# Two-stage token mix on one core: another entry into the first round, paced adds of x, DRAM adds moved, casts shared

## The chip, the cores and the metric

The kernel runs on one core of a Trainium2 chip. The metric is device time in microseconds. A core has a matrix engine (TensorE, called PE in the profile, with its weight loads as PEld), a vector engine (VectorE, DVE), an activation engine (ScalarE, ACT), GpSimd (POOL) and a queue engine (SyncE, SP). Each runs its own instructions in order; they meet only in semaphores. Transfers are issued by SP, ACT and POOL.

## The reference

The input x has shape (8, 4224, 192): batch, sequence, channels. First comes a causal convolution over 7 positions with softmax weights per head. Its result, called x again, goes through a mix of channels, a mix of tokens and another mix of channels:

```python
theta = x @ w_theta
zr, zi = x * cos(theta), x * sin(theta)
y = einsum('ts,bsd->btd', w_tok_r, zr) + einsum('ts,bsd->btd', w_tok_i, zi)
u = x + y
out = u + maximum(u @ w_ch, 0)
```

The token mix is by far the largest part: two matrices of 4224 x 4224, each applied to 1536 columns (batch times channel).

## The kernel before, in words

**Tiles.** The source tokens are cut into NK = 33 chunks of 128, the target tokens into NT = 33 blocks of 128. Two blocks make a unit, so there are NU = 17 units, the last with one block. In a pair, a scheme with seven products in place of eight is used: the weights of a pair of blocks give the tiles "11", "12", "21", "22" (turned by DVE, line 329) and the sums S1 to S4 (DVE, line 341); the chunk's z gives matching tiles Z11, T1, T2 and so on (products at line 248, sums at line 254).

**Steps.** The kernel is a sequence of NSTEP = 58 steps. A step works on one unit and on all chunks that are active in it. Chunk k is active for 17 steps from `start[k]`, so it meets every unit once. At most NW = 11 chunks are active at a time: the 33 chunks pass in three rounds of 11. `base` says in which step of its round each chunk enters, and `self.n` is the number of active chunks of a step:

```python
base = [0, 0, 1, 1, 2, 3, 3, 4, 4, 5, 5]
start = [base[k % NW] + (NU + 1) * (k // NW) for k in range(NK)]
```

In the first steps n is therefore 2, 4, 5, 7, 9, 11. A step has seven runs, one for each product tile; a run is n pairs of matmuls (line 429). After a run, `give` adds the PSUM result into the block's partial sum pv, on DVE (line 394), or copies it there on ACT (line 392) where it is a first visit. There are two PSUM tiles for the runs, so a later run waits until an earlier one has been given. Partial sums go to DRAM (`part`, two arrays used in turn) at the end of a step and come back when their unit is next visited (`load_rows`, line 365).

**A chunk's way in.** `load_chunk` fetches x (POOL queue, line 194, and SP for the overlap with the chunk before, line 185). `conv` is PE with ACT (lines 207, 148), and writes x to the DRAM array `xs`. `transpose` goes over PE; the copy out of PSUM is DVE's for chunks 0 to 2, ACT's for later ones. `theta` is PE (line 138) and two sines on ACT (line 243). Then come `product` and `sums` on DVE.

**The order** is written out by hand. Each engine's instructions are chained in program order. Inside a step, `mix` takes events (time in units of a run, action) and issues them between the pairs. The weights of step t+1 are turned and summed during step t (`w_tasks`: turns at 0.25, 1.2, 2.2, 4.2, sums at 2.05, 3.05, 3.3, 5.1). Their loads from DRAM (`load_w`, POOL, line 316) are issued in step t-1, into two stage buffers `st`, one for each weight matrix, so a load waits until the turns that read the buffer before it are done.

**The head** is the loop over i in the last part of the kernel. It brings in chunks 0 to 10, issues chunk i's convolution and chunk i-1's theta, products and sums, and fills in up to 11 pairs of the mix per iteration (`more`), as far as their chunks are ready; in iterations 1 and 2 it also issues matmuls on zeros (`idle`, line 571). The weights of step 0 are turned in iteration 1, ahead of the first transposed chunk's products:

```python
steps[0].load_rows()
for m in (1, 2):
    steps[0].load_w(m)
load_chunk(2)
for m in (1, 2):
    steps[1].load_w(m)
```

**Adding x.** u = x + y needs x added once to every block. For 24 blocks `add_x` loads x into xr (SP, line 375) and POOL adds it to pv in SBUF (line 376). For 9 blocks that are finished in the last steps (`self.late`) POOL issues accumulating transfers from `xs` into `part` in DRAM (line 381, two halves each), four steps before the block's last visit.

**The end of a block.** In its last visit pv is cast to 16 bits (ACT, line 451), transposed by a crossbar transfer issued by ACT (`cross_u`, line 155), or over PE in the late steps, multiplied by w_ch on PE (line 138), combined on DVE (line 464) and sent out by SP.

Of the kernel before, what the change touches and what calls it, by code (L numbers as in the profile page):

```python
# [9 lines left out]
AT = mybir.ActivationFunctionType  # L10
# [6 lines left out]
def kernel(  # L17
# [43 lines left out]
    NW = 11  # L61
    PC = 512

    base = [0, 0, 1, 1, 2, 3, 3, 4, 4, 5, 5]
    assert len(base) == NW
# [4 lines left out]
    NOSYNC = mybir.DependencyInfo(  # L70
        mybir.DependencyClass.NoSync, mybir.DependencyReason.DATA
    )
    last = {}

# [207 lines left out]
    class Step:  # L282


        def __init__(self, t):
            self.t, self.u, self.ks = t, unit(t), active(t)
            self.n = len(self.ks)
            self.tbs = [tb for tb in (2 * self.u, 2 * self.u + 1) if tb < NT]
            self.pair = len(self.tbs) == 2
            self.first = t < NU  # L290
            self.final = t + NU >= NSTEP
            self.late = self.final and self.n < NW
            self.ahead = self.late or 0 <= t + NU - NSTEP < 2
            visits = [v for v in range(NU, NSTEP) if v % NU == t % NU]
            self.adds = []
# [7 lines left out]
            self.st, self.w, self.ub, self.uT, self.pv = {}, {}, {}, {}, []  # L303

        def known(self, tb):

# [51 lines left out]
        def load_rows(self):  # L358
            for tb in self.tbs:
# [7 lines left out]
                    )  # L367
                self.pv.append(pv)

        def add_x(self, i):  # L370

            rows = slice(self.tbs[i] * P, (self.tbs[i] + 1) * P)
            if not self.ahead:
                xr = wk.tile([P, N], F16, name="xr", tag="xr", bufs=1)
                nc.sync.dma_start(out=xr, in_=xs[rows, :])
                pool(nc.gpsimd.tensor_tensor(  # L376
                    out=self.pv[i], in0=self.pv[i], in1=xr, op=ALU.add
                ))
                return
# [66 lines left out]
        def cast(self, i, g):  # L446
            if g == 0:
                self.ub[i] = wk.tile([P, N], F16, name="ub", tag="ub", bufs=2)
                self.uT[i] = turned()
            cols = slice(g * GC, (g + 1) * GC)  # L450
            act(nc.scalar.activation(  # L451
                out=self.ub[i][:, cols], in_=self.pv[i][:, cols], func=AT.Copy
            ))

        def turn_u(self, i, g):
            transposed(self.uT[i], self.ub[i], [g])
# [268 lines left out]
```

## Time and profile before

| What | Value |
|---|---|
| time, median of 9 runs | 1463.19 us |
| lowest and highest | 1455.8 and 1468.85 us |
| profiled execution, its own time | 1455.8 us |
| its span, first to last instruction | 1454.0 us |
| PE busy | 1418.5 us, 98% of the span |
| DVE busy | 1017.5 us, 70% |
| POOL busy | 435.6 us, 30% |
| ACT busy | 317.4 us, 22% |
| mean granted TensorE clock | 0.997 |
| DMA | 281.98 MB, mean 194 GB/s |

A busy engine is one with an instruction in flight. PE can be busy and still slow, since its matmuls overlap: the mean of one in a row is its latency, and the rate is read from how many there are in a stretch. A row of the page names line, engine, operation, output and inputs, shape and count; after the bar come the busy time, the mean of one in ns, the idle time of the engine just before and what ended it. In a timeline a row is start, length, engine, line, operation, count, and in brackets the idle time before it and its releaser. A window row gives, for each engine, the busy time in that stretch and in parentheses the number of instructions.

### The profile page before, as it was taken

Reading aid. Unit: us, or ns where it says so; the run is one execution under the profiler, and the core shown is the slowest. Engines: PE = TensorE matmul, PEld = TensorE weight load, DVE = VectorE, ACT = ScalarE, POOL = GpSimd, SP = SyncE. Lnnn points to the kernel's source line nnn. Section 1 sums busy time; section 2 is a strip of 40 time slices with the busy share of each in tenths; the row PEclk is TensorE's granted clock in tenths of the full one; section 3 lists DMA queues with packets and bytes.
Section 4 is the critical chain, followed back from the end, with each engine's and each line's share of the span. In section 5 each row is a group of like instructions: output and inputs, shape, how many; then the busy total and the mean of one; then the engine's idle time right before and its main releaser. Section 6 shows DMA issues by size and latency. Waiting matters only on the chain.

```text
span 1454.0 us, 23744 instructions
## 1 busy us (share of the span) xinstructions
PE 1418.5 (98%) x9809; PEld 888.3 (61%) x9809; DVE 1017.5 (70%) x1048; ACT 317.4 (22%) x382; POOL 435.6 (30%) x655
## 2 busy tenths in 40 slices
PE   7899999999999999999999999999999999999997
PEld 4556666666666666666656556666566666666565
DVE  6893554555458687867777757876788688677585
ACT  5861101111134244000000004335200100110134
POOL 8431211111223322532322443233133123234220
PEclk9999999999999999999999999999999999999999
DMA  9986756564699999897878889989889999999984
GB/s 172 233 174 139 145 116 134 98 151 89 153 229 210 223 236 241 207 260 152 242 167 195 225 147 242 227 197 237 211 184 209 214 200 205 235 255 205 252 207 139
DMA packets 272028, 281.98 MB, mean 194 GB/s; under 512 B 106672, under 2 KB 240176, under 8 KB 271920
## 3 DMA queue, kind: packets, MB, share of 16 engines
q0 software_dynamic: 162464, 92.15, 48.2%
q1 hardware_dynamic: 71824, 178.88, 35.2%
q10 hardware_dynamic: 37632, 9.44, 4.5%
q8 instruction: 77, 1.26, 0.3%
q14 instruction: 31, 0.25, 0.1%
HBM read 245.49 MB, written 108.13 MB: 243 GB/s over the span
## 4 chain that ended last, share of the span: by engine, by line
PE 85%; DVE 6%; DMA 3%; ACT 2%; issue 1%; POOL 1%; DVEq 0%; SPq 0%; ACTq 0%; POOLq 0%
PE y L429 78%; PE v L138 5%; DVE wt L341 2%; PE pc L207 1%; DMA uT<-ub 1%; PE tp L162 1%; ACT z L243 1%; DVE pv L394 1%; DVE wt L329 1%; DMA xw<-in_x_dram 1%; DVE z L254 1%; POOL st L316 1%; DVE z L248 1%; ACT uT L148 0%; DMA xs<-z 0%
## 5 line engine op out<-in xcount | busy, mean ns | idle before, releaser
L429 PE MATMUL y<-z,wt 128*128 128x384 f16 x7656 | 1285.0, 326 | 12.9 <-DVE pv L394 9.7
L429 PEld LDWEIGHTS <-wt 128*128 128x128 f16 x7656 | 741.0, 98 | 491.8 <-issue 14.2
L394 DVE TENSOR_TENSOR pv<-y,pv 128x768 f32<-128x768 f32 x324 | 308.5, 953 | 299.2 <-PE y L429 259.7
L329 DVE STREAM_TRANSPOSE wt<-st 128x1408 f16<-128x1408 f16 (+7 forms) x224 | 327.8, 1465 | 45.8 <-PE y L429 39.1
L316 POOL DMA_DIRECT2D st<-in_moe_w_tok_r_dram x232 | 132.8, 579 | 465.4 <-DVE wt L329 449.9
L316 POOL DMA_DIRECT2D st<-in_moe_w_tok_i_dram x232 | 132.7, 579 | 465.2 <-DVE wt L329 448.8
L341 DVE TENSOR_TENSOR wt<-wt 128x1408 f16<-128x1408 f16 (+7 forms) x216 | 218.8, 1013 | 40.7 <-PE y L429 38.2
L148 ACT ACTIVATE z<-pc 128x768 f16<-128x768 f32 x65 | 53.2, 819 | 389.4 <-PE pc L207 389.1
L451 ACT ACTIVATE ub<-pv 128x768 f16<-128x768 f32 x66 | 52.5, 836 | 343.7 <-DVE pv L394 327.5
L392 ACT ACTIVATE pv<-y 128x768 f32<-128x768 f32 x66 | 54.0, 818 | 281.8 <-PE y L429 281.8
L138 PEld LDWEIGHTS <-uT 128*128 128x128 f16 x1056 | 91.5, 98 | 29.5 <-issue 8.0
L194 POOL DMA_DIRECT2D xw<-in_x_dram x132 | 76.3, 584 | 28.1 <-DMA xw<-xw 7.7
L464 DVE SCALAR_TENSOR_TENSOR pv<-v,pv 128x768 f32<-128x768 f32 x66 | 62.8, 953 | 24.3 <-PE v L138 22.8
L376 POOL TENSOR_TENSOR pv<-pv,xr 128x1536 f32<-128x1536 f32 x24 | 74.7, 3111 | 17.1 <-issue 12.1
L254 DVE TENSOR_TENSOR z<-z 128x768 f16<-128x768 f16 x132 | 73.4, 556 | 3.6
L148 ACT ACTIVATE uT<-tp 128x1536 f16<-128x1536 f16 (+1 forms) x48 | 58.2, 1215 | 66.3 <-PE tp L162 66.3
L243 ACT ACTIVATE z<-v,half_pi 128x768 f16<-128x768 f32 x66 | 59.8, 906 | 41.9 <-PE v L138 41.5
L248 DVE TENSOR_TENSOR z<-z 128x1536 f16<-128x1536 f16 x66 | 60.0, 948 | 7.1 <-ACT z L243 7.1
L138 PE MATMUL v<-wch,uT 128*128 128x192 f16 x528 | 54.9, 248 | 4.8 <-DMA uT<-ub 2.9
L138 PE MATMUL v<-wth,uT 128*128 128x192 f16 x528 | 55.0, 248 | 4.5 <-ACT z L243 3.0
L243 ACT ACTIVATE z<-v 128x768 f16<-128x768 f32 x66 | 53.4, 810 | 0.0
L207 PE MATMUL pc<-xw,bands 96*64 96x192 f16 x528 | 35.5, 257 | 2.3 <-ACT bands L614 1.1
(43 smaller groups left out, 140.8 us busy)
## 6 DMA issues: line engine op xcount, KB each, us to landing
part<-pv SPq DMA_DIRECT2D x79, 768.0 KB, 4.2
pv<-part SPq DMA_DIRECT2D x79, 768.0 KB, 6.0
out_dram<-pv SPq DMA_DIRECT2D x66, 384.0 KB, 5.2
st<-in_moe_w_tok_r_dram POOLq DMA_DIRECT2D x136, 176.0 KB, 5.8
st<-in_moe_w_tok_i_dram POOLq DMA_DIRECT2D x136, 176.0 KB, 4.8
xs<-z SPq DMA_DIRECT2D x132, 96.0 KB, 4.4
xw<-in_x_dram POOLq DMA_DIRECT2D x121, 96.0 KB, 6.2
xr<-xs SPq DMA_DIRECT2D x24, 384.0 KB, 4.5
```

The source lines that it names most:

```text
L138: pe(nc.tensor.matmul(v[:, k, b * D : (b + 1) * D], lhsT=tT[:, 3 * k + b + i, :], rhs=w[:, 2 * b + i, :], start=(i == 0), stop=(i == 1),))
L148: act(nc.scalar.activation(out=out, in_=in_, func=AT.Copy))
L194: nc.gpsimd.dma_start(out=self.xw[lo : lo + n, h, :, :], in_=x[:, t0 : t0 + n, :].rearrange("b s d -> s b d"),)
L243: act(nc.scalar.activation(**args))
L248: dve(nc.vector.tensor_tensor(out=o, in0=xv, in1=o, op=ALU.mult))
L254: dve(nc.vector.tensor_tensor(out=z[:, o, :], in0=z[:, a, :], in1=z[:, b, :], op=ALU.subtract))
L316: pool(nc.gpsimd.dma_start(out=st[a * Q : (a + 1) * Q, 0:nb, :, 0:n] .rearrange("i r bt s -> i (r bt) s"), in_=w[self.tbs[0] * P : (self.t ...
L329: dve(nc.vector.transpose(self.w[name][:, 0 : self.n, :, :], self.st[int(name[1])][:, int(name[0]) - 1, :, 0 : self.n * Q] .rearrange("p b ...
L341: dve(nc.vector.tensor_tensor(out=self.w[name][:, 0 : self.n, :, :], in0=self.w[a][:, 0 : self.n, :, :], in1=self.w[b][:, 0 : self.n, :, : ...
L376: pool(nc.gpsimd.tensor_tensor(out=self.pv[i], in0=self.pv[i], in1=xr, op=ALU.add))
L394: dve(nc.vector.tensor_tensor(out=o, in0=yv, in1=o, op=ALU.add))
L429: pe(nc.tensor.matmul(y[cn][:, q, 0:BH], lhsT=self.w[wn][:, c, :, :].rearrange("p bt i -> p (bt i)"), rhs=chunks[k].z[:, zn, q * BH : (q + ...
```

## The change

There are five edits.

1. `base` has a list for each round. The first round enters over five steps, three chunks at once in the first (n is 3, 5, 7, 9, 11); the second has another order of its six steps. NSTEP stays 58.
2. Ahead of the head's loop, x of chunk 2 is fetched before step 0's weights, and x of chunk 3 before step 1's. Step 0's weights are turned at the end of iteration 1, after the sums of chunk 0.
3. POOL's add of x in SBUF is split from the load of xr, and given a semaphore wait on the DVE instruction that precedes it in program order; both are issued at other points of the step.
4. The accumulating transfers into DRAM are issued elsewhere: for blocks whose x is complete by step 23, in steps 27 to 35 and into the array that is read one visit earlier; for the others in step 41.
5. In the last two steps the cast of the first half of pv goes to DVE.

```diff
-    base = [0, 0, 1, 1, 2, 3, 3, 4, 4, 5, 5]
-    start = [base[k % NW] + (NU + 1) * (k // NW) for k in range(NK)]
+    base = [[0, 0, 0, 1, 1, 2, 2, 3, 3, 4, 4],
+            [0, 0, 1, 1, 2, 2, 3, 3, 4, 4, 5],
+            [0, 0, 1, 1, 2, 3, 3, 4, 4, 5, 5]]
+    start = [base[k // NW][k % NW] + (NU + 1) * (k // NW) for k in range(NK)]
...
-            self.ahead = self.late or 0 <= t + NU - NSTEP < 2
+            quiet = [v for v in visits if start[2 * NW - 1] < v <= 2 * NU]
+            self.adds, self.ahead = [], []
             for i, tb in enumerate(self.tbs):
-                at = [v for v in visits if self.known(tb) < v - 1 and v + NU < NSTEP
-                      and NU + 1 + base[-1] < v <= 2 * NU]
-                at = at[0] if at else visits[-1]
-                if t == at:
-                    self.adds.append(i)
+                known = self.known(tb)
+                if t not in ([v for v in quiet if known < v - 1] or visits[-1:])[:1]:
+                    continue
+                if not self.late:
+                    self.adds.append(i)
+                else:
+                    far = known <= start[2 * NW - 1]
+                    self.ahead.append((i, 2 * NU - NW + 2 * (t % NU) if far else start[-1],
+                                       (t // NU - 1 - far) % 2))
...
+        def load_x(self, i):
+            self.xr[i] = wk.tile([P, N], F16, name="xr", tag="xr", bufs=1)
+            nc.sync.dma_start(
+                out=self.xr[i], in_=xs[self.tbs[i] * P : (self.tbs[i] + 1) * P, :]
+            )
         def add_x(self, i):
+            ins = pool(nc.gpsimd.tensor_tensor(
+                out=self.pv[i], in0=self.pv[i], in1=self.xr[i], op=ALU.add
+            ))
+            tc.add_manual_dep(ins.ins, last["dve"].ins.name, SYNC, reason="pace")
+        def add_ahead(self, i, which):
+            tb = self.tbs[i]
             for cols in (slice(0, HN), slice(HN, N)):
                 pool(nc.gpsimd.dma_start(
-                    out=part[(self.t // NU - 1) % 2][self.tbs[i], :, cols],
-                    in_=xs[rows, cols], accum_op=ALU.add,
+                    out=part[which][tb, :, cols], in_=xs[tb * P : (tb + 1) * P, cols],
+                    accum_op=ALU.add,
                 ))
...
-            act(nc.scalar.activation(
-                out=self.ub[i][:, cols], in_=self.pv[i][:, cols], func=AT.Copy
-            ))
+            evacuate(self.ub[i][:, cols], self.pv[i][:, cols], self.t >= NSTEP - 2 and g == 0)
...
-            if not steps[t + 1].ahead:
-                for i in steps[t + 1].adds:
-                    found.append((3.3 + 1.7 * i, lambda i=i: steps[t + 1].add_x(i)))
-        for s in steps[t:]:
-            if s.ahead and t == s.t - (4 if s.late else 10):
-                for i in s.adds:
-                    found.append((3.3 + 1.7 * i, lambda s=s, i=i: s.add_x(i)))
+            for i in steps[t + 1].adds:
+                found.append((2 + 2 * i, lambda i=i: steps[t + 1].load_x(i)))
+                found.append((3.6 + 2 * i, lambda i=i: steps[t + 1].add_x(i)))
+        here = [(r, i, which) for r in steps for i, when, which in r.ahead if when == t]
+        for j, (r, i, which) in enumerate(here):
+            found.append((1.5 + 1.8 * j, lambda r=r, i=i, which=which: r.add_ahead(i, which)))
...
     steps[0].load_rows()
+    load_chunk(2)
     for m in (1, 2):
         steps[0].load_w(m)
-    load_chunk(2)
+    load_chunk(3)
     for m in (1, 2):
         steps[1].load_w(m)
...
-        if i == 1:
-            for _, f in steps[0].w_tasks():
-                f()
         if i + 3 < NW:
             load_chunk(i + 3)
...
             old.sums(1)
+        if i == 1:
+            for _, f in steps[0].w_tasks():
+                f()
         between(1)
```

On the queues this gives: on POOL, x of chunks 0, 1, 2, step 0's two weight loads, x of chunk 3, step 1's weight loads, x of chunks 4 to 6. On DVE, in the head: the copies of chunks 0's and 1's transposed x, products and sums of chunk 0, all turns and sums of step 0, the first turn of step 1, the copy of chunk 2's transposed x. On SP the overlap of chunk 3 comes ahead of three of the four stores of chunk 0's x. PE has the same number of instructions of every kind.

More of the change, by code (lines that the diff above doesn't have):

```diff
@@ L62 @@
     PC = 512
-    base = [0, 0, 1, 1, 2, 3, 3, 4, 4, 5, 5]
-    assert len(base) == NW
-    start = [base[k % NW] + (NU + 1) * (k // NW) for k in range(NK)]
+    base = [[0, 0, 0, 1, 1, 2, 2, 3, 3, 4, 4],
+            [0, 0, 1, 1, 2, 2, 3, 3, 4, 4, 5],
+            [0, 0, 1, 1, 2, 3, 3, 4, 4, 5, 5]]
+    assert all(len(b) == NW for b in base)
+    start = [base[k // NW][k % NW] + (NU + 1) * (k // NW) for k in range(NK)]
     NSTEP = start[-1] + NU
@@ L71 @@
         mybir.DependencyClass.NoSync, mybir.DependencyReason.DATA
+    )
+    SYNC = mybir.DependencyInfo(
+        mybir.DependencyClass.Sync, mybir.DependencyReason.SCHED_ONLY
     )
@@ L292, in __init__ @@
             self.late = self.final and self.n < NW
-            self.ahead = self.late or 0 <= t + NU - NSTEP < 2
             visits = [v for v in range(NU, NSTEP) if v % NU == t % NU]
-            self.adds = []
+            quiet = [v for v in visits if start[2 * NW - 1] < v <= 2 * NU]
+            self.adds, self.ahead = [], []
             for i, tb in enumerate(self.tbs):
-                at = [v for v in visits if self.known(tb) < v - 1 and v + NU < NSTEP
-                      and NU + 1 + base[-1] < v <= 2 * NU]
-                at = at[0] if at else visits[-1]
-                if t == at:
+                known = self.known(tb)
+                if t not in ([v for v in quiet if known < v - 1] or visits[-1:])[:1]:
+                    continue
+                if not self.late:
                     self.adds.append(i)
+                else:
+                    far = known <= start[2 * NW - 1]
+                    self.ahead.append((i, 2 * NU - NW + 2 * (t % NU) if far else start[-1],
+                                       (t // NU - 1 - far) % 2))
             self.time = 0.324 * self.n * (7 if self.pair else 4)
-            self.st, self.w, self.ub, self.uT, self.pv = {}, {}, {}, {}, []
+            self.st, self.w, self.xr, self.ub, self.uT, self.pv = {}, {}, {}, {}, {}, []
         def known(self, tb):
@@ L368, in load_rows @@
                 self.pv.append(pv)
-        def add_x(self, i):
[L372 to L377, printed above, removed]
-                ))
-                return
+        def load_x(self, i):
+            self.xr[i] = wk.tile([P, N], F16, name="xr", tag="xr", bufs=1)
+            nc.sync.dma_start(
+                out=self.xr[i], in_=xs[self.tbs[i] * P : (self.tbs[i] + 1) * P, :]
+            )
+        def add_x(self, i):
+            ins = pool(nc.gpsimd.tensor_tensor(
[4 more added lines that the diff above has]
+            tb = self.tbs[i]
             for cols in (slice(0, HN), slice(HN, N)):
                 pool(nc.gpsimd.dma_start(
-                    out=part[(self.t // NU - 1) % 2][self.tbs[i], :, cols],
-                    in_=xs[rows, cols], accum_op=ALU.add,
+                    out=part[which][tb, :, cols], in_=xs[tb * P : (tb + 1) * P, cols],
+                    accum_op=ALU.add,
                 ))
@@ L450, in cast @@
             cols = slice(g * GC, (g + 1) * GC)
-            act(nc.scalar.activation(
-                out=self.ub[i][:, cols], in_=self.pv[i][:, cols], func=AT.Copy
-            ))
+            evacuate(self.ub[i][:, cols], self.pv[i][:, cols], self.t >= NSTEP - 2 and g == 0)
         def turn_u(self, i, g):
```

## The prediction

> **What bounds the kernel now.** I read the page from the engine shares down, then the waits, then single stretches. TensorE (PE) is busy for 98% of the span, and the first two lines say with what: 7656 matmuls of the token mix. The third is what feeds them.
>
> ```profile
> PE 1418.5 (98%) x9809; PEld 888.3 (61%) x9809; DVE 1017.5 (70%) x1048; ACT 317.4 (22%) x382; POOL 435.6 (30%) x655
> L429 PE MATMUL y<-z,wt 128*128 128x384 f16 x7656 | 1285.0, 326 | 12.9 <-DVE pv L394 9.7 <-ACT pv L392 1.7 <-DMA xw<-xw 1.2
> L341 DVE TENSOR_TENSOR wt<-wt 128x1408 f16<-128x1408 f16 (+7 forms) x216 | 218.8, 1013 | 40.7 <-PE y L429 38.2
> ```
>
> The change leaves the number of PE instructions of every kind as it is (the mix keeps 7656), so only time lost around them can be won: 1454.0 - 1418.5 = 35.5 us idle, and matmuls that run slow. Windows of 20 us place the idle time: 17.6 us before 120 us (the head), 9.5 after 1400 (the end), 8.4 in between. The rest of the span runs 125 mix matmuls per 20 us, 161 ns each.
>
> In between, the PE timeline names two kinds of stall. The first belongs to the adds of x on POOL:
>
> ```profile
> 726.73 4.55 DVE L341 TENSOR_TENSOR wt<-wt 128x1408 f16<-128x1408 f16 x1
> 727.41 3.12 POOL L376 TENSOR_TENSOR pv<-pv,xr 128x1536 f32<-128x1536 f32 x1
> ...
> 733.73 8.45 PE L429 MATMUL y<-z,wt 128*128 128x384 f16 x51 [0.82 <-DVE pv L394]
> ```
>
> A weight sum that elsewhere takes 0.88 us takes 4.55 while POOL adds; the partial sums queued behind it are late, and PE waits 0.82. The same happens at 809 (0.76) and 835 (0.82): 2.4 us in all. The second is a crossbar transfer of u:
>
> ```profile
> 1329.87 5.56 ACTq L155 DMA_TRANSPOSE uT<-ub  x1
> ...
> 1349.35 1.46 PE L138 MATMUL v<-wch,uT 128*128 128x192 f16 x8 [2.94 <-DMA uT<-ub]
> ```
>
> It lands after 19.4 us. Windows show landings of 3.2 to 8.0 us (medians) up to 1240, and 7.5 to 19.4 from 1240 on, when the DRAM adds of L381 run. The clock then falls to 0.78 (window 1350 to 1355): the 8 matmuls take 1.46 instead of 0.82, the next 16 take 3.56 instead of 2.76. Together 2.94 + 0.64 + 0.80 = 4.4 us.
>
> In the head DVE is the tight engine: 18.2 of 20 us busy in 20 to 40, 19.5 in 60 to 80.
>
> ```profile
> 16.36 2.29 POOL L316 DMA_DIRECT2D st<-in_moe_w_tok_r_dram  x4 [1.47 <-DVE wt L329]
> ...
> 24.64 0.70 DVE L329 STREAM_TRANSPOSE wt<-st 128x512 f16<-128x512 f16 x1
> 25.54 0.96 DVE L146 COPY uT<-tp 128x1536 f16<-128x1536 f16 x1 [0.20 <-PE tp L162]
> ...
> 104.19 20.98 PE L429 MATMUL y<-z,wt 128*128 128x384 f16 x128 [2.46 <-DVE pv L394]
> ```
>
> POOL can fetch step 1's weights only once DVE has turned step 0's (two stage buffers). Here that was at 16 us, so the data lay ready when DVE turned them at 24.64.
>
> **What the Trainium skill says.** SBUF - State Buffer, "Who interferes with whom": a DVE instruction with two SBUF inputs contends with a GpSimd instruction that reads SBUF, and whoever comes second blocks wholly. The trace agrees: L341 is held 3.7 us, while the partial sums of L394 (one input in PSUM) keep 0.96 under the same add. DMA: Bandwidth & Descriptors, "Issuing engines are not separate DMA queues": what SP, ACT and POOL issue shares 16 DMA engines; the crossbar's landings agree. TensorE: Matmul & The Clock Gate, "What's actually happening": after an idle window of some 3.4 us the clock halves; here an idle 2.94 already led to a mean of 0.78.
>
> **The change part by part.**
>
> *Adds paced.* All 24 POOL adds stay, 3.11 us each. Each now waits for the last DVE instruction before it in program order (S2 or S4). A unit of step time is 11 x 0.324 = 3.56 us: the first add at 3.6 meets the next weight sum at 5.1, 5.3 us on; the second at 5.6 meets the next step's first sum at 2.05, over 12 us on. Turns and partial sums in between don't block. Behind the waiting add on POOL stands only a fetch of weights for two steps ahead, and SP's load of the second xr, one buffer, waits for the first add (1 us at most before 4.0). Gain: the three stalls, -2.4. Bounds 0 (another late input) to -3.
>
> *Adds in DRAM moved.* The 18 DMAs of L381 stay. Five tiles go to steps 27 to 35, four to step 41, before the first crossbar transfer except its last halves. Their issue is 18 x 0.87 = 16 us of an otherwise idle POOL queue, ahead of fetches with a step of slack: nothing. Gain -4.4. Bounds 0 (the late stage is simply busy, DMA share 1.15) to -4.4 here.
>
> *Shared casts.* Three casts of the last two steps go to DVE. The nearest row is the 128x384 cast (374 ns); twice that is 0.75, against ACT's 0.83. PE's waits for ub after 1440 are 0.61 and 0.45; DVE still has an output in line. I take -0.6, bounds -1.1 to +0.7.
>
> *Round transitions.* The second round now enters under n = 8 at steps 17 to 21 (9 or 10 before), some of the third too. Such a step holds PE 14 x 8 x 0.161 = 18.0 plus two chunks of 3.3, 24.6 us; DVE 7 x 0.95 + 4 x 1.21 + 4 x 0.68 + 8.2 (products and sums of two chunks) = 22.4: 91%, where n = 9 gives 88%. PE lost 0.73 twice there. I take +0.7, bounds -0.7 to +5.
>
> *The head.* Step 0 has three chunks, so its runs are 0.97 us instead of 0.65 and PE waits less for gives (1.13, 1.23, 0.78 before). xw of chunk 2 comes first on POOL, and of chunk 3 ahead of step 1's weights: the 0.67 wait at 27.27 goes. But step 0's turns move behind chunk 0's sums, so they begin at 24.65, not 15.3. A 128x384 turn should be 0.56 (0.43 at 256, 0.70 at 512), so the second ends at 25.75; POOL then takes 0.3 + 2.3 to issue step 1's real weights, and the last lands after 3.8 (the row at 16.36): 31.7. DVE has finished step 0's weights by 28.1, and next in its order is the first turn of step 1; the copy of chunk 2's transposed x stands behind it. So DVE idles 3.6 us and that copy moves from 25.54 to 32.5. Chunk 4's xw stands behind both weight fetches on POOL, lands at 38, and is just in time.
> From there I walk the queues. ACT has 5.75 us per chunk plus 0.7 per copy of a partial sum; PE per iteration 11 pairs x 0.323 + 3.3 = 6.9. Chunk 4's sines start at 49.7 (46.9 before), chunk 5's at 57.4 (54.7); then PE's 7 us beats before's 7.1 to 8.2, chunk 9's start at 85.1 (84.1), and free running starts at 93.3 (92.8), with 81 pairs done instead of 85: 0.5 + 4 x 0.323 = 1.8 behind. DVE owes more there: with steps of 5, 7 and 9 chunks it has turned 9-chunk weights by pair 105. I get waits of 1.1 and 2.9 against before's 2.46 at 104: +1.6 more. PE also idles 28.6 to 33.5, longer than any gap of the head now; from 30 to 45 before the clock was 0.81 to 0.90, so I add 1.0. Head: 1.8 + 1.6 + 1.0 = +4.4. Bounds: -6 (two thirds of the 8.8 us that PE waits in the head for gives, xw and sums, by its timeline, vanish and no new wait comes) to +16 (below).
>
> Sum on the profiled execution (1455.8 us, span 1454.0 and 1.8 around it): -2.4 - 4.4 - 0.6 + 0.7 + 4.4 = -2.3, so **1453.5**. It is the lowest of nine; the median 1463.19 is 7.4 above it. What can differ by microseconds between executions is where DMAs meet: the crossbar against the adds is the only place where the trace shows such a lottery (7.5 to 19.4 us). I take most of the excess, 6 of 7.4, to go with it: 1453.5 + 1.4 = 1454.9, say **1455**.
>
> **The rivals.**
> *The head gains.* For it: waits for gives fall with fewer, longer runs, and DVE's work up to the first 11-chunk turn is the same (79.7 against 79.1 us by counting rows). Then -6 instead of +4.4: 1444.5. Against: the late fetch, which the order of the queues dictates.
> *A wash.* The excess of the median lies elsewhere (clock, HBM) and stays: 1453.5 + 7.4 = 1461. For it: the nine runs spread over 13 us and only one was profiled. If the late stage is merely busy, add 4.4: 1465.
> *Slower: DVE starves on step 1's weights.* Place: the first turn of step 1 in the head. If the fetch lands after 8.8 us (the longest in the head) instead of 3.8, +5; if each of the six later iterations then takes 8.2 (the longest now) instead of 7.1, +6.6; the head costs 16 and the execution stands at 1465, or 1472 with the median's excess. It decides from a head loss of about 15. For it: DVE is the tight engine. Against: few transfers run then, and later iterations have slack on PE.
> *It doesn't do what it says:* last halves of the adds of step 41 may still meet the first crossbar transfers near 1049; those have 12 us of slack, so 0.
>
> **How the numbers follow.** Likeliest case 0.50 (1447 to 1462), the head gains 0.20, a wash 0.20, slower 0.10. Half a percent (7.3 us) is about what can be told from no change: faster means below 1455.9, slower above 1470.5. The first case straddles 1455.9 and gives 0.29 faster and 0.21 same, the wash is same but for 0.01 faster: faster 0.50, same 0.40, slower 0.10. The range holds all but the outer tails: 1439 to 1469.
>
> **What would show it.** Right: no PE wait on uT<-ub near 1349 and landings of at most 12 us; no L341 above 2 us; PE waits on DVE gone at 733, 809, 835; DVE idle around 28 to 32 on st, first sines of chunk 4 near 50. Wrong: DVE turns step 1's weights by 26; free running starts below 90 or beyond 97; waits above 1 us at n = 8.

## The result, and the profile after

The changed kernel takes **1470.27 us** (median of 17 runs, 1467.26 to 1477.33). The kernel before, run beside it, takes 1459.21 us (median of 54, 1450.51 to 1470.81). The ratio is 1.0078, with a 95% interval of 1.0059 to 1.0097: slower by 11 us. The forecast was 1455 us, a gain; the result is a loss and lies just above the forecast's range (1439 to 1469). Two executions of the kernel before, at 1473.2 and 1479.62 us, were in a slower state and are counted in no range below.

The profiled execution of after took 1467.75 us with a span of 1466.0, 12.0 more than the span of before. Its page, engine shares first, then the groups that answer to those shown of before (columns: busy us, mean ns of one, idle us just before):

```profile
PE 1421.3 (97%) x9809; PEld 890.0 (61%) x9809; DVE 979.5 (67%) x1051; ACT 315.6 (22%) x379; POOL 435.3 (30%) x655
...
L445 PE MATMUL y<-z,wt 128*128 128x384 f16 x7656 | 1283.9, 326 | 15.2 <-DVE pv L410 10.7
...
L350 DVE TENSOR_TENSOR wt<-wt 128x1408 f16<-128x1408 f16 (+8 forms) x216 | 175.8, 814 | 46.8 <-PE y L445 44.6
```

The third line is good news: a weight sum now takes 814 ns in the mean instead of 1013. The second has PE idle 15.2 us ahead of the mix instead of 12.9. The waits of PE in after (us in total, times, longest) name what is new:

```profile
PE y L445 <- DVE pv L410: 10.7, 14, 2.8
PE pc L212 <- ACT z L153: 6.2, 1, 6.2
PE v L143 <- DVE uT L151: 4.0, 1, 4.0
...
PE y L445 <- DVE wt L338: 2.5, 1, 2.5
```

The last three stand in the head. 4.0 stands where the forecast had PE idle, and 2.5 where it had step 0's turns late. 6.2 had not been forecast: it is one wait of a convolution for ACT. The timeline of after shows the forecast part first (start, length, engine, line, operation; in brackets the idle time before it and its releaser):

```profile
25.58 2.29 POOL L325 DMA_DIRECT2D st<-in_moe_w_tok_r_dram  x4 [8.30 <-DVE wt L338]
...
32.19 0.84 DVE L338 STREAM_TRANSPOSE wt<-st 128x640 f16<-128x640 f16 x1 [4.36 <-DMA st<-in_moe_w_tok_r_dram]
32.96 0.92 DVE L151 COPY uT<-tp 128x1536 f16<-128x1536 f16 x1
...
33.93 1.46 PE L143 MATMUL v<-wth,uT 128*128 128x192 f16 x8 [3.98 <-DVE uT L151]
```

POOL gets the fetch of step 1's weights out only at 25.58, when DVE has turned step 0's. DVE idles 4.36 us for them, and the copy of chunk 2's transposed x stands behind. Then comes the part that was not forecast:

```profile
79.84 0.34 SPq L458 DMA_DIRECT2D part<-pv  x1
...
86.23 0.81 ACT L153 ACTIVATE z<-pc 128x768 f16<-128x768 f32 x1 [7.93 <-DMA part<-pv]
...
87.09 0.85 PE L212 MATMUL pc<-xw,bands 96*64 96x192 f16 x8 [6.17 <-ACT z L153]
```

ACT can't write chunk 9's z before a **store of a partial sum** has landed, 6.3 us after SP issued it. The code says why: z has a pool of NW = 11 buffers, and `load_rows` (`if self.t < 2`) takes the partial sums of steps 0 and 1 from it as well. With noise (the zeros of `idle`), four partial sums and eleven z, chunk 9 gets the buffer of step 1's first partial sum. Step 1 has five chunks now instead of four; with step 0's 21 pairs its last pair is the 56th, not the 42nd. Chunk 9's convolution comes behind pair 54, so it now stands ahead of the end of step 1; in before it came behind pair 58, long after it. The same store and the same z in before:

```profile
70.07 0.83 SPq L442 DMA_DIRECT2D part<-pv  x2
...
76.31 0.94 ACT L148 ACTIVATE z<-pc 128x768 f16<-128x768 f32 x1
```

There the first store landed after 3.5 us, at 73.6, and z was written with 2.7 us to spare.

Where the 12.0 us of span lie:

| Part | us |
|---|---|
| head: pair 112 of the mix starts at 117.6 (113.06 + 14 x 0.323) instead of 104.19 | +13.4 |
| PE idle 440 to 620: 4.12 instead of 0.73; 900 to 1060: 3.51 instead of 2.15 | +4.8 |
| waits on DVE at 733, 809, 835: gone | -2.4 |
| wait on uT at 1349 and the slow matmuls behind it: gone | -4.4 |
| PE waits in the last two steps: 3.5 instead of 3.2 | +0.3 |
| sum | +11.7 |

### The profile page after: what moved, and what is told of

Its sections match the earlier page's. It is cut to its first block, busy times and chain, and to the rows that moved or that the text cites. A ratio compares the mean times of both kernels' runs of the same rounds, so it can differ in the third digit from the quotient of the medians.

```text
span 1466.0 us, 23742 instructions
## 1 busy us (share of the span) xinstructions
PE 1421.3 (97%) x9809; PEld 890.0 (61%) x9809; DVE 979.5 (67%) x1051; ACT 315.6 (22%) x379; POOL 435.3 (30%) x655
## 4 chain that ended last, share of the span: by engine, by line
PE 84%; DVE 8%; DMA 3%; ACT 3%; issue 1%; SPq 0%; POOL 0%; DVEq 0%; ACTq 0%
PE y L445 76%; PE v L143 5%; DVE pv L410 2%; DVE z L253 2%; DVE z L259 2%; ACT z L248 2%; PE pc L212 1%; PE tp L167 1%; DVE wt L338 1%; DVE wt L350 1%; DMA xw<-xw 1%; DMA xs<-z 1%; DVE pv L478 0%; DMA xw<-in_x_dram 0%; DMA part<-pv 0%
## 5 line engine op out<-in xcount | busy, mean ns | idle before, releaser
L445 PE MATMUL y<-z,wt 128*128 128x384 f16 x7656 | 1283.9, 326 | 15.2 <-DVE pv L410 10.7
L338 DVE STREAM_TRANSPOSE wt<-st 128x1408 f16<-128x1408 f16 (+8 forms) x224 | 327.6, 1465 | 46.2 <-PE y L445 41.5
L350 DVE TENSOR_TENSOR wt<-wt 128x1408 f16<-128x1408 f16 (+8 forms) x216 | 175.8, 814 | 46.8 <-PE y L445 44.6
L253 DVE TENSOR_TENSOR z<-z 128x1536 f16<-128x1536 f16 x66 | 60.4, 951 | 13.8 <-ACT z L248 13.6
```

Of the source, the lines that this page charges most:

```text
L253: dve(nc.vector.tensor_tensor(out=o, in0=xv, in1=o, op=ALU.mult))
L338: dve(nc.vector.transpose(self.w[name][:, 0 : self.n, :, :], self.st[int(name[1])][:, int(name[0]) - 1, :, 0 : self.n * Q] .rearrange("p b ...
L350: dve(nc.vector.tensor_tensor(out=self.w[name][:, 0 : self.n, :, :], in0=self.w[a][:, 0 : self.n, :, :], in1=self.w[b][:, 0 : self.n, :, : ...
L445: pe(nc.tensor.matmul(y[cn][:, q, 0:BH], lhsT=self.w[wn][:, c, :, :].rearrange("p bt i -> p (bt i)"), rhs=chunks[k].z[:, zn, q * BH : (q + ...
```

## The experiments

"Pair 112" below is read as in the table, so kernels with different entries can be compared. The kernel before ran beside every group, with medians of 1459.2 to 1461.4 us; a comparison of kernels from two groups carries that much doubt.

**1. Which edits lose: undo 1 and 2, or do them alone.** The first kernel is after with these lines as before:

```diff
-    base = [[0, 0, 0, 1, 1, 2, 2, 3, 3, 4, 4],
-            [0, 0, 1, 1, 2, 2, 3, 3, 4, 4, 5],
-            [0, 0, 1, 1, 2, 3, 3, 4, 4, 5, 5]]
+    base = [[0, 0, 1, 1, 2, 3, 3, 4, 4, 5, 5]] * 3
...
     steps[0].load_rows()
-    load_chunk(2)
     for m in (1, 2):
         steps[0].load_w(m)
-    load_chunk(3)
+    load_chunk(2)
...
+        if i == 1:
+            for _, f in steps[0].w_tasks():
+                f()
         if i + 3 < NW:
```

> The changed kernel with edits 1 and 2 undone: base and the head's order of the kernel before, edits 3, 4 and 5 kept. My theory: the loss lies in the entry alone (head and transitions), and the paced and moved adds gave what the trace of after shows, 2.4 + 4.4, with the casts at 0. Then this kernel is 6 to 8 us faster than before (ratio 0.995 to 0.996), its free running starts near 92.8 us as before, and no PE wait above 1 us stands between 600 and 900 or on uT<-ub from 1240 to 1420. Rival A: the stalls of the adds were a matter of one execution, and edits 3 to 5 move no time on average: ratio 0.999 to 1.001. Rival B: part of the 12 us lost comes from edits 3 to 5 (DMAs of the adds in steps 27 to 41): slower than before by up to 3 us.

The second is the kernel before with the reverse of that.

> The kernel before with edits 1 and 2 alone (bases of three lists, new order of loads, step 0's turns late). My theory: the whole loss is here, 13.4 in the head and 4.8 in the transitions, so this kernel is about 18 us slower than before (ratio 1.012 to 1.013), free running starts near 103 us, chunk 9's z waits some 8 us on DMA part<-pv. Rival B (edits 3 to 5 carry part of the loss): 11 us slower or less.

Measured: edits 3 to 5 alone **1448.41** us (1447.47 to 1450.46; ratio 0.9932, interval 0.9909 to 0.9956), edits 1 and 2 alone **1482.28** us (1472.38 to 1488.84; ratio 1.0165, 1.0129 to 1.0201). So the entry costs 22.0 us on its own, where 18 was expected, and 1470.27 - 1448.41 = 21.9 on top of the others, and edits 3 to 5 gain 12 either way. Rivals A and B fall. The gain is larger than I expected, and the spread of 20 us has shrunk to 3 (six runs); experiment 4 takes that up. In the profile of edits 1 and 2 alone, the slowest of its six runs (1488.84 us), chunk 9's conv waits 6.66 us for z, as expected, and three waits on crossbar transfers (11.8 us) come on top.

The kernel with edits 3 to 5 alone is also the answer to what beats both: 11.9 us under before and 21.9 under after.

**2. Two waits of the head, one at a time and together.** Partial sums of step 1 from the other pool:

```diff
-                if self.t < 2:
+                if self.t < 1:
                     pv = zpool.tile([P, N], F32, name="pv", tag="z")
                 else:
                     pv = wk.tile([P, N], F32, name="pv", tag="big", bufs=6)
```

> The changed kernel, but the two partial-sum tiles of step 1 come from the pool of the later steps' partial sums instead of z's pool of 11 buffers, so that chunk 9's z need not wait for step 1's store to DRAM. My theory: the ACT wait of 7.9 us ahead of chunk 9's z (PE 6.2) goes, and with it the cold clock from 80 to 100 us: 7 to 9 us faster than after, so 2 to 4 us slower than before; free running starts near 95. Rival C: that wait only covered another one (ACT's sines, DVE's products, the late fetch); taking it away wins under 3 us and PE waits for another engine between 80 and 100. Rival D: the tiles taken from the other pool make the xw loads or steps 2 to 4 wait for buffers: the head keeps its 13 us with a PE or ACT wait on another DMA.

After with the loads and the place of step 0's turns of before (the last two parts of the first diff), the five-step base kept:

> The changed kernel with edit 2 alone undone: the old order of loads, step 0's turns in iteration 1 ahead of chunk 0's products; the five-step base and all else kept. My theory: DVE's 4.4 us of idling at 32 us (on st) and PE's waits of 2.5 and 4.0 us between 22 and 34 go, but chunk 9's z still waits for the store of step 1's partial sum, since step 1 still has five chunks; iterations that start some 4 us earlier do not bring step 1's end forward by more. 2 to 5 us faster than after, the wait ahead of chunk 9's z stays between 5 and 10 us. Rival E: the late fetch is the root, it delays step 1's end and with it the store; then the z wait falls below 2 us here and the kernel is 8 us or more faster than after. Rival F: the late turns pay for something (chunk 2's xw early): 0 to 2 us slower than after.

Both:

> Both single mends of the head together: edit 2 undone, and step 1's partial-sum tiles from the other pool; five-step base kept. My theory: they are two waits one after the other (5 to 6 us of late fetch and cold clock at 22 to 37 us, 6 us of z wait near 80), so their gains add: 5 to 7 us faster than either alone, about 1455 to 1457 us; pair 98 ends near 100 us, as in the kernel before. What then is left against the kernel with edits 1 and 2 undone (1448.4) is 6 to 8 us, nearly all of it in the transitions (n = 8). Rival G: after the first wait is gone the head is bound by DVE (19.3 of 20 us busy in 40 to 60), so the second mend brings under 2 us: about 1461. Rival H: the five-step entry then pays, and pair 98 ends by 97.

| Kernel | median (range), us | pair 112, us | against before |
|---|---|---|---|
| after | 1470.27 (1467.26 to 1477.33) | 117.58 | +13.4 |
| step 1's pv from the other pool | 1461.44 (1459.42 to 1468.07) | 109.60 | +5.4 |
| step 0's turns early, loads as before | 1463.87 (1461.57 to 1469.01) | 110.33 | +6.1 |
| both | 1454.98 (1453.42 to 1464.71) | 102.81 | -1.4 |

The gains are 8.8 and 6.4, and together 15.3: they add, as two waits in a row do. Rival C (another wait stands behind it), D, F, G fall. Rival E falls too: with the early turns the store goes out 7.4 us earlier (72.45) and chunk 9's conv begins to wait 7.0 us earlier (73.94), so the wait is still 5.83. Rival H, that the shorter entry then pays, holds for the head: pair 98 ends at 95.5, by the 97 that it named, PE waits 2.79 us for DVE behind it, and pair 112 stands 1.4 us ahead of before and 2.1 ahead of the kernel with edits 3 to 5 alone (104.91). It doesn't hold for the whole: 1454.98 us is 6.6 above that kernel. So in the head the five-step base by itself gains 2.1 us, and the loss comes from edit 2 and the buffer. The two halves of edit 2, the loads and the turns, were not taken apart.

What the buffer cost beyond its 6.2 us shows in the window of 80 to 100 us, in after (busy time and number for PE, PEld, DVE, ACT, POOL; then PEclk, DMA share, GB/s):

```profile
80.00:100.00 20.00, 13.67 (x120) 9.24 (x118) 11.26 (x16) 12.82 (x17) 2.34 (x4) 0.83 0.60 163
```

and the same window of the kernel with the other pool:

```profile
80.00:100.00 20.00, 18.50 (x162) 12.10 (x160) 18.19 (x25) 16.62 (x21) 2.88 (x5) 1.00 0.80 198
```

PE does 120 matmuls there instead of 162, at a clock of 0.83 instead of 1.00. The Trainium skill (TensorE: Matmul & The Clock Gate, "What's actually happening") has the clock fall after an idle window of some 3.4 us; the wait of 6.17 us and the mean of 0.83 agree.

**3. The transitions: is it n?** The kernel with both mends, with the second and third list as before:

```diff
-            [0, 0, 1, 1, 2, 2, 3, 3, 4, 4, 5],
+            [0, 0, 1, 1, 2, 3, 3, 4, 4, 5, 5],
             [0, 0, 1, 1, 2, 3, 3, 4, 4, 5, 5]]
```

> The kernel of the run before with base's second and third list set to those of the kernel before; the first keeps its five steps. n is then 8, 8, 8, 8, 7, 7, 9 in steps 17 to 23 instead of 8, 8, 8, 8, 8, 10, 11, and 9, 9, 10, 9, 9, 9 in steps 35 to 40 as in the kernel before. My theory: the transition's loss follows n, because DVE's work per step (7 gives, 8 turns and sums, two chunks' products and sums) does not shrink with n as PE's does. So between 900 and 1050 PE's idle time falls from 5 to about 2.1 us as with edits 1 and 2 undone, while between 440 and 620 it grows, from 3.3 to 5 to 9 us at n = 7. Net 0 to 4 us slower than the kernel of the run before. Rival I: the loss comes from where the chunks enter (two per step, every step) and not from n: then 480 to 600 stays at 3.3 and the kernel is 3 us faster.

Measured: 1458.84 us (1456.41 to 1463.77), 3.9 slower than with after's lists. Windows over the two transitions, columns as above, for edits 3 to 5 alone (n of 9 and 10 in both):

```profile
440.00:620.00 180.00, 179.07 (x1333) 113.13 (x1331) 141.87 (x161) 58.81 (x67) 61.56 (x95) 1.00 0.97 223
900.00:1060.00 160.00, 157.86 (x1187) 99.43 (x1185) 122.11 (x140) 57.84 (x66) 52.53 (x88) 1.00 1.04 238
```

for after's lists with both mends (n of 8, and 8 or 9):

```profile
440.00:620.00 180.00, 175.88 (x1339) 111.40 (x1337) 143.83 (x171) 66.26 (x75) 60.61 (x98) 1.00 1.03 239
900.00:1060.00 160.00, 156.49 (x1181) 98.23 (x1179) 124.56 (x148) 60.12 (x69) 55.51 (x94) 1.00 1.06 240
```

and for this kernel (n of 8 and 7, and 9 or 10):

```profile
440.00:620.00 180.00, 171.77 (x1311) 108.85 (x1309) 142.82 (x171) 66.50 (x76) 60.85 (x99) 1.00 1.03 238
900.00:1060.00 160.00, 157.86 (x1192) 99.31 (x1190) 123.20 (x144) 58.96 (x68) 53.75 (x91) 1.00 1.03 236
```

PE's idle time (the width less the first number) is 0.93, 4.12 and 8.23 in the first transition, and 2.14, 3.51 and 2.14 in the second: it follows n in both. (In the second, this kernel has the lists of before, so only the first tells n from the places of entry.) Rival I, which expected 3 us less and no more idle time in the first, falls. In a step with n = 8 the same pair of waits comes back each time, here from the timeline of after's lists with both mends:

```profile
471.58 0.82 PE L143 MATMUL v<-wth,uT 128*128 128x192 f16 x8 [0.16 <-ACT z L248]
486.53 0.48 PE L445 MATMUL y<-z,wt 128*128 128x384 f16 x2 [0.54 <-DVE pv L410]
```

That n = 8 follows from the five steps: the chunks that came in early go out early, and step 17 is left with eight. So the shorter entry is paid for here even where both waits of the head are gone: 4.6 us in these windows, against the 2.1 that the head gains. The spans of the two profiles differ by 3.4 us; what makes 6.6 of it in the medians stays open.

**4. Why edits 3 to 5 gain 12 us and not 6.8.** One edit at a time; edit 3 alone, then edit 4 alone:

> The kernel before with edit 3 alone (load of xr split off, add of x paced by a semaphore on DVE). My theory: the three waits on DVE at 733, 809 and 835 go, no weight sum takes over 2 us, 2.4 us faster than before, and the times still spread over some 15 to 20 us, since the crossbar transfers still meet the adds in DRAM. Rival J: the sums lose their holds but the partial sums are late all the same: 0.

> The kernel before with edit 4 alone (adds in DRAM in steps 27 to 35 and 41). My theory: edits 3 to 5 together gave 11.9 us at the median and shrank the spread from 20 to 3 us; 2.4 is edit 3's, so 8 to 10 us of it is this edit's, of which the profiled execution of before, a fast one, showed only 4.4. The spread falls to 3 to 5 us. Rival K: the spread of before comes from elsewhere (clock, weights' DMAs against POOL's adds) and stays over 12 us; the gain is 4 us or less.

Measured: edit 3 alone 1449.92 us (1448.97 to 1450.43; ratio 0.9911, 0.9876 to 0.9946), edit 4 alone 1452.18 us (1449.06 to 1454.81; ratio 0.9934, 0.9909 to 0.9960). Edit 4 gained the 9 us that I expected (8 to 10), with a spread a little wider (5.8 for 3 to 5). **Edit 3 did not** do as expected: it was to bring 2.4 and leave the spread, and brought 11.3 and took the spread away. The two gains don't add, so both may remove the same thing. Edit 3 also turns an order on POOL: in one step near 1300 us, the two accumulating transfers that stood behind the adds in SBUF go ahead of them. Edits 3 and 4 together, without 5:

> Edits 3 and 4 alone: before's entry, and the casts of the last two steps left on ACT. My theory, from the traces: sharing the casts moved nothing (PE's waits after 1440 us were 3.2 before and 3.5 after), so this kernel equals the one with edits 3, 4 and 5 (1448.4) within 0.7 us. The prediction's figure was 0.6 us in favour of sharing; the rival is a loss of up to 0.7 by sharing.

gave 1448.95 us (1447.12 to 1451.06), against 1448.41 with the casts shared; with ranges of 3 and 4 us nothing can be told from this. To see whether that order counts, with the adds unpaced as in the kernel before:

```diff
-                    found.append((3.3 + 1.7 * i, lambda s=s, i=i: s.add_x(i)))
+                    found.append((3.2 + 1.7 * i, lambda s=s, i=i: s.add_x(i)))
```

> The kernel before with one number changed: the late blocks' DRAM adds stand at 3.2 + 1.7 i in the step instead of 3.3 + 1.7 i. This changes POOL's order in one step alone (near 1300 us), where an accumulating transfer then goes ahead of the add of x in SBUF instead of behind it, and is issued some 3 us earlier, ahead of the crossbar transfers at 1326 and 1330. My theory, from the kernel with edit 3 alone (11 us faster, spread 1.5): most of the spread of before comes from this one meeting, and edit 3 had removed it by turning the same order. Then this kernel is 5 to 9 us faster than before at the median, with a spread of 5 to 10 us, without touching the stalls at 733, 809, 835; the crossbar lands within 12 us. Rival L: the gain of edit 3 beyond 2.4 comes from other places (the holds of DVE by unpaced adds in other executions): then 0 to 2 us faster, spread as before.

Measured: 1452.53 us (1450.39 to 1454.31; ratio 0.9942, 0.9927 to 0.9957). One number, two adds of POOL behind two accumulating transfers instead of ahead of them, and 8.9 us; the stalls of 0.8 us at 735, 811 and 837 are all there. Rival L (the unpaced adds make the spread) falls here; what is left against edit 3 alone, 2.6 us, is about the stalls (3.2 us in this profile). The reverse is to bring the wait back with paced adds. First the accumulating transfers are put behind the adds again (4.1 in place of 3.3 in the same line):

> The kernel with edit 3 alone, but with the late blocks' DRAM adds at 4.1 + 1.7 i: in the same one step the accumulating transfers stand behind POOL's paced adds again, as in the kernel before, and the second is issued at about 1325 us, where the crossbar transfers start. My theory: the wait of PE on uT from the crossbar near 1345 comes back in part of the executions: 4 to 9 us slower than with edit 3 alone (1449.9), spread 10 us or more. Rival L: 1449 to 1451 with a spread of 2 us, since the adds stay paced.

gave 1448.87 us (1447.25 to 1450.87): no loss, where 4 to 9 us were expected. The second accumulating transfer went out at 1324.20, 1.7 us ahead of the first crossbar transfer, not 0.4 as in before. Next it is put at 6.9 and held back by a semaphore on DVE:

```diff
+                if meet:
+                    tc.add_manual_dep(ins.ins, last["dve"].ins.name, SYNC, reason="pace")
```

> The kernel with edit 3 alone, but in the one step near 1300 us the second block's accumulating transfer is held to 6.9 runs by a semaphore on DVE, so that POOL issues it at about 1326 us, beside the first crossbar transfer of u and ahead of the second (in the kernel before it went out 0.4 us before the first). So far: issued 5.2, 4.6 and 1.7 us ahead of the first crossbar transfer the crossbar landed within 12 us and the times spread by 1.5 to 4 us; issued 0.4 us ahead it landed after 19.4, with a spread of 20 and more. Theory: what counts is that the accumulating transfer is under way while crossbar transfers are, so the wait on uT near 1345 comes back: 1453 to 1460 us, spread over 8, a landing above 13 us in the profile. Rival L: the spread of before came from the unpaced adds in SBUF after all; then 1449 to 1451, spread under 4.

It went out at 1323.87, still 1.3 us ahead of the first crossbar transfer, and the time was 1449.56 us (1448.39 to 1450.70): again no loss, where 1453 to 1460 was expected. Both times are those that rival L named. Two more executions of the kernel before were profiled:

> The kernel before itself, to see another of its executions than the one profiled at 1455.8 us, which was among its fast ones (median 1460). Theory: the excess over some 1450 us lies in PE waits on uT from crossbar transfers between 1240 and 1400 us, of 3 us or more each, with the cold clock after them; an execution at 1460 has two of them or one of 8 us. Rival L: it lies between 600 and 900 us, in more or longer waits on DVE than the three of 0.8 us.

> As the run before it: the kernel before, another execution. Theory and rival as there.

They took 1450.62 and 1458.38 us. Both have the waits on DVE of 0.8 us (near 733, 809 and 835). The first has no wait on uT; the second is in this timeline (the accumulating transfer, the two crossbar transfers, and PE's wait for the second):

```profile
1325.72 1.77 POOL L381 DMA_DIRECT2D part<-xs  x2
1326.13 2.06 ACTq L155 DMA_TRANSPOSE uT<-ub  x1
1329.90 8.64 ACTq L155 DMA_TRANSPOSE uT<-ub  x1
...
1351.20 1.46 PE L138 MATMUL v<-wch,uT 128*128 128x192 f16 x8 [4.78 <-DMA uT<-ub]
```

So three executions of the kernel before, 1450.6, 1455.8 and 1458.4 us, have PE waiting 0, 2.94 and 4.78 us for the same transfer. In the third it is more than one transfer that is late. From 1336 to 1346 us the DMA engines move 79 GB/s, where they move 288 in the first (columns as above; the first execution, then the third):

```profile
1336.00:1346.00 10.00, 10.00 (x74) 6.70 (x73) 7.40 (x9) 0.00 (x0) 1.40 (x3) 1.00 1.16 288
1336.00:1346.00 10.00, 10.00 (x71) 6.39 (x69) 7.77 (x8) 0.00 (x0) 1.39 (x2) 1.00 1.87 79
```

The next accumulating transfers, issued at 1335.61, land after 19.2 us instead of 8.8, and the fetch of weights at 1333.28 after 16.1 instead of 7.5. The accumulating transfer of 1325.72 itself lands at the start of the stretch, after 9.6 us. Last, the paced kernel with the accumulating transfer held into the next step, at two points:

> As the kernel with the paced adds whose accumulating transfer was to meet the crossbar transfers, which in fact went out at 1323.87 us, 1.3 us ahead of the first of them: here it is held to 0.05 runs into the next step, so about 1325.5 to 1326.5 us, beside the first crossbar transfer and ahead of the second, as in the kernel before. Two of three executions of the kernel before lost 2.9 and 4.8 us of PE to the second crossbar transfer (issued 1329.9, landing after 19.4 and 21.2 us), the third nothing. Theory (the meeting makes the spread): some executions lose 3 us and more again: highest minus lowest 7 us or more, median 1451 to 1458. Rival: other traffic of that stretch that the unpaced add also delays (the load of step weights at 1320.5, the store at 1322) decides, not this transfer; then 1449 to 1451 with a spread under 4 us.

> The same, held to 0.6 runs into the next step, about 1327.5 to 1329 us, between the two crossbar transfers. Theory: as in the run before it, or worse, since the accumulating transfer then lies wholly under the second crossbar transfer, the one that was late: spread 7 us or more, median 1451 to 1460. Rival: 1449 to 1451, spread under 4.

The first gave 1454.93 us (1451.67 to 1465.03, 22 runs), as expected. The second gave 1449.91 us (1447.01 to 1451.73, 13 runs), where 1451 to 1460 was expected and the rival said 1449 to 1451. The timeline of the first:

```profile
1322.09 1.57 ACTq L158 DMA_TRANSPOSE uT<-ub  x1
1324.33 1.71 POOL L389 DMA_DIRECT2D part<-xs  x2 [3.88 <-DVE pv L404]
1325.67 6.18 ACTq L158 DMA_TRANSPOSE uT<-ub  x1
...
1346.13 1.46 PE L141 MATMUL v<-wch,uT 128*128 128x192 f16 x8 [3.90 <-DMA uT<-ub]
```

The wait is back with paced adds: 5.0 us at the median against the second kernel, which ran beside it, and a spread of 13. All points together (issue of the second accumulating transfer against the second crossbar transfer, and the longest landing of a crossbar transfer from 1240 us on, both in the profiled execution; the range is that of all runs, with their number):

| Kernel | ahead of the second by, us | longest landing, us | range of times, us (runs) |
|---|---|---|---|
| edit 3 alone | 8.8 | 10.5 | 1448.97 to 1450.43 (6) |
| order turned, not paced | 8.2 | 9.9 | 1450.39 to 1454.31 (6) |
| paced, behind | 5.3 | 11.7 | 1447.25 to 1450.87 (6) |
| paced, held to 6.9 | 4.9 | 11.2 | 1448.39 to 1450.70 (12) |
| before (three profiles) | 4.0 to 4.2 | 19.4, 11.0, 21.2 | 1450.51 to 1472.63 (200) |
| paced, next step at 0.05 | 1.3 | 20.4 | 1451.67 to 1465.03 (22) |
| paced, next step at 0.6 | 0.05 | 9.5 | 1447.01 to 1451.73 (13) |

This shows that the place of this transfer decides on the loss, and that pacing the adds doesn't prevent it: of four places with paced adds one lost. It also corrects the picture: to be under way together is not enough, the points from 1.3 to 4.2 us ahead lose, and of three profiled executions at 4.0 to 4.2 one did not. Nor is the distance a rule. In the profile of edits 1 and 2 alone one crossbar transfer with the accumulating transfer 4.0 us ahead lands after 19.5 us, but two later ones land after 13.8 and 21.8 with the last accumulating transfer 4.2 and 11.4 us ahead (the next goes out 1.4 us behind the second of them, and this one costs PE most):

```profile
1409.48 1.46 PE L140 MATMUL v<-wch,uT 128*128 128x192 f16 x8 [8.16 <-DMA uT<-ub]
```

What slows the DMA engines in such a stretch was not shown.

## Why the prediction was wrong, and where it was right

**The head: the step that failed.** It put +4.4. Against the kernel with the same edits 3 to 5 and the old entry (pair 112 at 104.91) the head of after costs 117.58 - 104.91 = 12.7. The walk was nearly right in what it listed. DVE idled 4.36 us where 3.6 were put; the copy of chunk 2's x started at 32.96 where 32.5 was put; the two waits for gives are 1.00 and 2.79 where 1.1 and 2.9 were put. With step 1's partial sums in the other pool, free running starts at 95.4 where 93.3 was put, and the rest of after's head costs 109.60 - 104.91 = 4.7, next to the +4.4. What the walk left out is a **buffer**: it followed each engine's queue and both stage buffers of `st`, and not the pool of z, which holds the partial sums of steps 0 and 1. Five chunks in step 1 make it end at pair 56, behind chunk 9's convolution, and chunk 9 waits for its store: 12.7 - 4.7 = 8.0 us in the profiles, 8.8 in the medians. Nothing new had to be measured to see it. `load_rows` names the pool, and before's trace has the store landing at 73.6 and chunk 9's z at 76.31: 2.7 us of slack, for a step that was to end 14 pairs (4.5 us of mix alone) later.

The rival on the slower side had a price near the measured one by luck, for another mechanism: it put 16 us on the head if step 1's weights came late. They came within 0.5 us of the time forecast (first turn at 32.19, forecast 31.7). The rival that the head gains was right in part: without edit 2 and with the other pool it gains 2.1 us, not 6.

**Round transitions: mis-sized.** +0.7 was put, -0.7 to +5 as bounds. In the two windows after's lists idle 3.2 + 1.4 = 4.6 us more. I compared DVE's share of a step (91% against 88%) and took the wait of 0.73 as typical. At n = 8 waits of 0.54 and 0.16 appear in every step of the first transition, and one of 1.20 or 1.25 in each transition: a mean share under 100% doesn't price an order in which partial sums stand behind products.

**Adds paced: right in what it named.** The three waits are gone, -2.4. The Trainium skill (SBUF - State Buffer, "Who interferes with whom") has a DVE instruction with two SBUF inputs contend with a GpSimd instruction that reads SBUF; the paced kernels agree, 805 to 817 ns for L350 and its like instead of 980 to 1020. The prediction adds from there that whoever comes second blocks; its own lines don't bear that out, since the sum starts 0.68 us ahead of the add (726.73 and 727.41) and is held all the same. What the prediction missed is that behind these adds on POOL stand accumulating transfers too, in one late step. In the change itself edit 4 takes them out of that step, so it cost the sum nothing; for edit 3 alone it is some 9 of its 11 us.

**Adds in DRAM moved: right.** -4.4 in the profile, and the guess that most of the median's excess goes with it held too. Edits 3 to 5 on before's profile are 1455.8 - 2.4 - 4.4 = 1449.0; the measured median is 1448.41, with no excess left. The skill's sentence that the queues share 16 DMA engines (DMA: Bandwidth & Descriptors, "Issuing engines are not separate DMA queues") fits: in the late execution the fetch of weights (16.1 us for 7.5) is late together with the crossbar transfer. Why the moment of issue decides, no run explains.

**Shared casts:** -0.6 was put; no run could tell it from 0.

**The sum.** Entry 12.7 + 4.6 = 17.3 us, which is the difference of the two spans (1466.0 and 1448.7). In the medians it is 21.9: after's median is 2.5 above its profiled execution, and the other kernel's 2.05 below its own. What makes the 2.5 stays open. Put for the two terms: +5.1.

**What was to show it.** The prediction's signs came, but for two: there is no wait on uT near 1349, the waits at 733, 809 and 835 are gone, and DVE idles around 28 to 32; chunk 4's sines begin at 51.4 instead of near 50, and one weight sum takes over 2 us:

```profile
636.02 3.10 POOL L388 TENSOR_TENSOR pv<-pv,xr 128x1536 f32<-128x1536 f32 x1 [8.65 <-DMA xr<-xs]
...
637.34 2.53 DVE L350 TENSOR_TENSOR wt<-wt 128x1408 f16<-128x1408 f16 x1
```

There the add waited for its xr, and not for the DVE instruction that was to pace it, so it met a sum after all; it cost PE nothing. Two signs of being wrong came as well. Free running beyond 97 pointed to the failure: it began at 103.4. A wait above 1 us at n = 8 pointed to the transitions: 1.20 at 578 us.

## What to carry to other kernels

When an order is changed, walk the buffers too: for each pool write down who takes the buffer of whom, and by when its last reader, a store for instance, is through. A start in fewer steps moves the end of early steps back and lowers n where the next round takes over (9 or 10 to 8 here), so price the transitions with the order of the engine that shares the step, not with its mean share. If a kernel's times spread by more than the change is worth, find the transfer that some executions wait for; an order turned on one queue gained 8.9 us here.

## What I had not expected of the hardware

Near 1340 us some executions have a stretch of some 10 us in which all DMAs are slow at once: 79 to 116 GB/s instead of 251 to 288, and a crossbar transfer of u that lands after 19.4 to 21.2 us instead of at most 11.7. It came in four of the five profiled executions in which an accumulating transfer into DRAM had been issued 1.3 to 4.2 us ahead of the second crossbar transfer, and in none of the five in which it had been issued 0.05 us or 4.9 us and more ahead; but one transfer, later in the slowest of these executions, took 21.8 us with the last one issued 11.4 us ahead. Executions of the kernel before, from 1450.6 to 1458.4 us, differ in large part by this wait; its slower ones, up to 1472.63, were not profiled.
